# Attention and maxout feed-forward on one core: a re-planned order from the first folds on, and filler copies in the lead

## The chip, the cores and the metric

The kernel runs on 1 of the 8 cores of a Trainium2 chip. The metric is device microseconds (us) of one execution on that core. Three runs of the kernel before took 160.72, 161.04 and 161.48 us; their median is 161.04 us. One further execution was profiled.

## What is computed

```python
a = softmax(phi, axis=seq)                      # 8 batches, 8 heads, 576 rows, 32 memory slots
k_m, v_m = einsum('bhsm,bhsd->bhmd', a, k), the same with v      # head size 64
attn = softmax(q @ k_m.T / 8)                   # 576 x 32 per head
x = (attn @ v_m), heads side by side            # 4608 x 512
h = max(x @ w1, x @ w2, x @ w3)                 # 4608 x 768
out = h @ w_out                                 # 4608 x 512, float32
```

## The kernel before

**The algebra.** `attn @ v_m @ w` is computed as `attn @ (v_m @ w)`: the small v_m of a batch is first multiplied into the weights (called a fold, `fold`, L462), and the attention weights then go through the folded weights (`ffn1`, L513). The maxout is computed on differences: w1-w3 and w2-w3 are folded, h is the maximum of the two results and 0, and the part x @ w3 @ w_out comes back through a third folded matrix made of w3 @ w_out (`w3_o`, L197). The subtractions of w3 are done in place in the weights (`w_diff`, L218); batch 0 is folded before them, with an extra matmul of minus w3.

**The stages of a batch.** Loads of phi, k, v and q; an exponential of phi (`att_exp`, ScalarE); products of it with k and v (`att_kv`, TensorE, L256); their normalising (`att_kv_norm`) and transposing (`att_kv_t`, L315); scores from the transposed q (`att_q` is the transpose on VectorE, `att_score` the matmuls L351 and an exponential on ScalarE); the second softmax by a transpose, a sum, a reciprocal, a multiply and a transpose back; four folds; twelve `ffn1` groups of four matmuls over 576 columns, of which the even ones end in a relu and the odd ones in a maximum on VectorE; and the second feed-forward. For batches 0 and 1 that is `ffn2` (begun by `ffn2_begin`, L672, four matmuls); for the others it is done with seven block products instead of eight (`products`, L624), whose sums of blocks (`combine`, L549) run on GpSimd or VectorE.

**The order.** Nothing is scheduled for the program: `manual_schedule` is on, and one long string of words is issued word by word (L810 to L840). A word is a letter, a number and a batch: `F10@0` is ffn1 group 10 of batch 0. Each engine runs its instructions in the order of the words. The letters used in the text: L loads (0 phi, 1 k, 2 v, 3 q), J half of a q, Y weights; E exponential of phi; B products with k and v (B0 for k and B1 for v in batches 0 and 1, without a number for both); N normalise; K transpose; Q transpose of q; S scores; a, s, c, m, X the second softmax; D folds; F ffn1; t and T begin and end of ffn2; V the subtraction of w3; U and A sums of blocks of the weights and of the activations (batch 9 stands for w_out itself); P products; r packing of k; g sending an output; Z warm-up matmuls. An exclamation mark swaps the engine: ScalarE against VectorE for what empties PSUM, VectorE against GpSimd for V, U, A and m, GpSimd against ScalarE for r.

**PSUM.** There are eight banks. Each word that writes PSUM takes the next digit of a string (L143); D, F, B, and S take pairs (S two pairs). A word can start on a bank only when its earlier contents have been read.

**Loads and packing.** All loads but the first phi are issued from GpSimd's queue (POOL), in the order of the words, and the same queue holds GpSimd's computing instructions, so a waiting instruction holds back the loads behind it. k is loaded densely (tile ko, two buffers) and packed with a column of ones into the tile kvr (three buffers), from batch 2 on, by `pack` (L107 on GpSimd, L105 on ScalarE). v is loaded into kvr itself, q into qq (two buffers).

```python
        if swap:
            nc.scalar.copy(out=out_, in_=in_)
        else:
            nc.gpsimd.tensor_copy(out=out_, in_=in_)
```

Of the kernel before, what the change touches and what calls it, by code (L numbers as in the profile page):

```python
# [9 lines left out]
BF16 = mybir.dt.bfloat16  # L10
# [5 lines left out]
def kernel(  # L16
# [12 lines left out]
    nc = tc.nc  # L29

    B, H, S, D = q.shape
    M = phi.shape[-1]
    P = 128
# [11 lines left out]
    const = ctx.enter_context(tc.tile_pool(name="const", bufs=1))  # L45
# [18 lines left out]
    K1 = NP * NC * KS  # L64
# [20 lines left out]
    def load_ph(b):  # L85
        ph = inp.tile([P, NP, NC, M], FP32, name="ph", tag="ph")
        loaded.setdefault(b, {})["ph"] = ph
        dst = ph.rearrange("p j c m -> p j (c m)")
        if b == 0:
            for h in halves:  # L90
                nc.sync.dma_start(out=dst[:, h], in_=by_pair(phi, b)[:, h])
        else:
            nc.gpsimd.dma_start(out=dst, in_=by_pair(phi, b))

    def load_kv(b, i, h=slice(0, NP)):
        kv = vs[b % 3] if i else ks[b % 2]
        nc.gpsimd.dma_start(  # L97
            out=kv[:, h].rearrange("p j c d -> p j (c d)"),
            in_=by_pair((k, v)[i], b)[:, h],
        )  # L100

    def pack(b, swap):
        out_, in_ = krs[b % 3][:, :, :, 0:D], ks[b % 2]
# [5 lines that stand above are left out]
    def load_q(b, h=slice(0, NP)):  # L109
        if "q" not in loaded.setdefault(b, {}):  # L110
            loaded[b]["q"] = inp.tile([P, NP, NC, D], BF16, name="qq", tag="qq")
        nc.gpsimd.dma_start(  # L112
            out=loaded[b]["q"][:, h].rearrange("p j c d -> p j (c d)"),
            in_=by_pair(q, b)[:, h],
        )

    def load_w(i):
        w = (moe_w1, moe_w2, moe_w3)[i]
        nc.gpsimd.dma_start(  # L119
            out=w_sb[:, :, i], in_=w.rearrange("(j p) f -> p j f", p=P)  # L120
        )
# [3 lines left out]
    def load_wo():  # L125
        nc.gpsimd.dma_start(out=wo_sb, in_=moe_w_out.rearrange("(t p) c -> p t c", p=P))
# [3 lines left out]
    warm = const.tile([P, BANK], BF16, name="warm")  # L130
# [7 lines left out]
    for i in range(P // M):  # L138
# [4 lines left out]
    banks = iter(  # L143
        "".join(
            """
            00232204420145545045026406426402640264023462467420742602462062460264024603604206
            42604620642164646240624607402604260240402402420724062042642024204204260424026427
            402742002442072420426045026520026265260602406243352
            """.split()
        )  # L150
    )
# [1 line left out]
    def one_bank():  # L153
        return psum[:, int(next(banks))]
# [5 lines left out]
    def warm_up(n):  # L160

        po = one_bank()
        for _ in range(n):
            nc.tensor.matmul(  # L164
                po[:, 0:BANK], lhsT=warm[:, 0:P], rhs=warm, start=True, stop=True
            )
# [46 lines left out]
    def w_diff(n, swap):  # L213

        c, end = [(0, BANK), (BANK, DF), (2 * BANK, 2 * DF), (DF, 2 * BANK)][n]
        while c < end:
            e = min(end, (c // DF + 1) * DF)
            (nc.gpsimd if swap else nc.vector).tensor_tensor(  # L218
                out=w12[:, :, c:e],
                in0=w12[:, :, c:e],  # L220
                in1=w_sb[:, :, 2, c % DF : c % DF + e - c],
                op=ALU.subtract,
            )
            c = e
# [202 lines left out]
    def att_rec(b, g):  # L427
        x = st[b]["ts"][:, groups(g)]
        nc.vector.reciprocal(out=x, in_=x)  # L429
# [302 lines left out]
    def ffn2_last(b, c0):  # L732
# [18 lines left out]
        for i, (c, po) in enumerate(zip(cs, pos)):  # L751
# [13 lines left out]
            else:  # L765
                nc.scalar.copy(out=ot[:, c], in_=po)
                nc.scalar.dma_start(out=rows, in_=ot[:, c])

    def issue(b, n, swap):

        i = int(n[1:]) if len(n) > 1 else None
        {
            "I": lambda: [make_identity(nc, ident)]
            + [nc.gpsimd.memset(x[:, :, :, D:], 1.0) for x in krs],
            "Y": lambda: load_w(i) if i < 3 else load_wo(),
            "L": lambda: load_ph(b) if i == 0 else load_q(b) if i == 3 else load_kv(b, i - 1),
            "J": lambda: load_q(b, halves[i]),
            "H": lambda: load_kv(b, i % 2, halves[i // 2]),
            "h": lambda: load_kv(b, 0, slice(i, i + 1)),
            "r": lambda: pack(b, swap),  # L780
            "E": lambda: [att_exp(b, h) for h in (halves if b == 0 else [slice(0, NP)])],
            "B": lambda: att_kv(b, i),
            "N": lambda: att_kv_norm(b, swap, i),
            "K": lambda: att_kv_t(b, swap, i),
            "Q": lambda: att_q(b, i),
            "S": lambda: att_score(b),
            "a": lambda: att_t(b, i),
            "s": lambda: att_sum(b, i),
            "c": lambda: att_rec(b, i),
            "m": lambda: att_mul(b, i, swap),  # L790
            "X": lambda: (ones_mul if (b, i) in ONES else att_back)(b, i),
            "M": lambda: ones_sum(b, i),
            "R": lambda: ones_rec(b, i),
            "D": lambda: fold(b, i, swap),
            "F": lambda: ffn1(b, i, swap),
            "T": lambda: ffn2(b, i, swap),
            "U": lambda: combine_w(b, i, swap),
            "A": lambda: combine_a(b, i, not swap),
            "P": lambda: products(b, i, swap),
            "W": lambda: w3_t(i, swap),  # L800
            "g": lambda: send(i),
            "d": lambda: fold_begin(i),
            "t": lambda: ffn2_begin(b, i),
            "O": lambda: w3_o(i, swap),
            "V": lambda: w_diff(i, swap),
            "Z": lambda: warm_up(i),
        }[n[0]]()


    for w in """  # L810
        E@0 h2@0 h3@0 h0@0 h1@0 L3@0 Z25@0 B0@0 Y2@0 I@0 N0@0 Z2@0 K0@0! Q0@0 Q1@0 Z9@0 S@0 Z2@0
        M0@0 M1@0 R0@0 R1@0 W0@0 Y3@0 W1@0 W2@0 Z6@0 O1@0 H3@0 O3@0 O2@0 H1@0 X1@0 B1@0
        X0@0 N1@0 K1@0 O0@0 Y0@0 D1@0! D0@0! D3@0 F10@0 F0@0! F8@0 Y1@0 L0@1 L1@1 J0@1
        F2@0! F6@0 V0@0! D4@0! D2@0 E@1 J1@1 F4@0! F1@0 F5@0 L2@1 F3@0 F7@0 F9@0 L3@2
        F11@0 B0@1 N0@1! t1@0 L1@2 t2@0 Q1@1 Q0@1 T2@0 K0@1! V1@0 V3@0 T1@0 S@1 L0@2
        B1@1 U0@9! N1@1! M1@1 a0@1 R1@1 t3@0 K1@1! T3@0 L2@2 s0@1 L1@3 c0@1 V2@0 D0@1
        D1@1! L0@3 D2@1 L2@3 t0@0 r0@2 X1@1 m0@1! X0@1 T0@0 F10@1! Q0@2 F6@1 E@2 F7@1
        F0@1 g2@0 F11@1 L3@3 F1@1 D3@1 Q1@2 F2@1 B@2 U1@9 F4@1 L1@4 L0@4 N@2 F3@1 F8@1
        K@2 g1@0 F5@1 L2@4 S@2 F9@1 D1@2! t3@1 E@3 D0@2 D2@2 D3@2 L3@4 a@2 T3@1 s@2 U3@9
        T4@1! c@2 m@2! r0@3 X@2 B@3 F0@2 U0@2 N@3 F8@2! F6@2 K@3 U1@2 Q0@3 L1@5 F2@2  # L820
        L0@5 Q1@3 U3@2 F10@2 g0@0 F3@2 F4@2 F9@2 F11@2 U2@9 S@3 a@3 s@3 t2@1 c@3 g3@0
        D3@3 D2@3 L2@5 U2@2 D0@3 U0@3 t0@1 r0@4! E@4 F1@2 T0@1! U1@3 F5@2 T2@1! F7@2
        t1@1 m@3 L3@5 A0@2! X@3 L0@6 T1@1! F6@3 F4@3! D1@3! B@4 N@4 L1@6 A1@2! F0@3 Q1@4
        F2@3 Q0@4 L2@6 A2@2! F8@3 K@4! F7@3 P1@2! F1@3 S@4 P2@2 F10@3 D0@4 a@4 D1@4!
        P0@2 A3@2! s@4 c@4 F3@3 P4@2 E@5 r0@5! F11@3 F9@3 m@4 F5@3 L3@6 P5@2 A0@3! T4@3!
        A1@3! D3@4 B@5 X@4 N@5 D2@4 Q1@5 Q0@5 P6@2 F2@4 K@5 P3@2 F10@4! S@5 L1@7 P1@3!
        D2@5 D1@5! a@5 F11@4 P2@3 F8@4 s@5 c@5 U2@3 L0@7 F4@4! F0@4 F6@4 r0@6! L2@7 P0@3
        F1@4 F7@4 F9@4 P4@3 E@6 A2@3! A3@3! F3@4 F5@4 P3@3 D0@5 m@5 L3@7 U3@3 D3@5 B@6
        A0@4! A1@4! X@5 N@6 P5@3 F6@5 F8@5! Q0@6 r0@7 F2@5 Q1@6 F10@5 K@6! F9@5 U0@5
        F4@5 F7@5 P6@3! S@6 E@7 F3@5 P1@4 a@6 F5@5 F11@5 P2@4 D0@6 U0@4 B@7 D3@6 U2@4  # L830
        N@7 s@6 P0@4 A2@4! F0@5 F1@5 Q1@7 K@7! U1@4 A3@4! P4@4 D1@6! A0@5! D1@7! c@6
        D2@7! m@6 P3@4! U3@4 P5@4! D0@7 D2@6 D3@7 U2@6 Q0@7 X@6 T4@5 S@7 A1@5! A3@5!
        P6@4! F10@6 a@7 F6@6 s@7 F4@6 F11@6 F0@6 F7@6 c@7 P1@5 P2@5 F2@6! U2@5 F5@6 F3@6
        P0@5 U1@5 F1@6 m@7 F8@6 A2@5! X@7 P4@5 P3@5 F4@7 U0@6 U1@6 F10@7 U3@5 F9@6 P5@5!
        F5@7 F8@7 A0@6! P1@6! A1@6! F2@7 F6@7 F0@7 P6@5! U0@7 F7@7 F3@7 F1@7 P2@6! F11@7
        F9@7 A0@7 P0@6 A2@6! A1@7 P4@6 A3@6 U3@6! P1@7 P2@7 A2@7 P5@6 P3@6 U2@7! U1@7
        P4@7 P0@7! A3@7 P6@6 U3@7! P5@7 P3@7! P6@7! T4@7!
    """.split():
        n, b = w.rstrip("!").split("@")
        issue(int(b), n, w.endswith("!"))  # L840


# [28 lines left out]
```

## Time and profile before

| | us |
|---|---|
| median of three runs | 161.04 |
| profiled execution | 160.76 |
| span of that execution | 159.0 |
| TensorE busy (matmuls) | 149.6 |
| VectorE busy | 116.8 |
| GpSimd busy | 109.2 |
| ScalarE busy | 98.8 |

The span is what the profiler sees of the program; the execution's own time has 1.8 us more around it. PE is TensorE's matmuls, PEld its weight loads, DVE VectorE, ACT ScalarE, POOL GpSimd, SP the queue that sends most outputs. Matmuls are pipelined: the record of a 288-column matmul lasts 0.29 us, but they start 0.12 us apart, so a group of four takes PE 0.49 us and its result is there about 0.17 us later. The granted TensorE clock was full (1.00) throughout. In a row of the timeline the number in brackets is the idle time of the engine before it and what ended that.

### The profile page before, as it was taken

How to read it: one execution, taken by the hardware profiler on the slowest of the kernel's cores; microseconds unless marked ns; L12 is line 12 of the kernel's file. 1: busy time of each engine (PE TensorE's matmuls, PEld its weight loads, DVE VectorE, ACT ScalarE, POOL GpSimd, SP SyncE). 2: the span in 40 equal slices, each digit the busy share in tenths (PEclk: the TensorE clock that was granted, in tenths of full speed). 3: DMA queues.
4: the chain of work that ended last, by engine and by line, in shares of the span. 5: the costliest groups of instructions: out<-in, count | busy, mean ns of one | idle time of the engine just before them, and what ended most of it. 6: DMA issues, size and time to landing. Idle time of an engine off the chain costs nothing.

```text
span 159.0 us, 5179 instructions
## 1 busy us (share of the span) xinstructions
PE 149.6 (94%) x2218; PEld 100.3 (63%) x2228; DVE 116.8 (73%) x203; ACT 98.8 (62%) x142; POOL 109.2 (69%) x101
## 2 busy tenths in 40 slices
PE   6987798999798999999999999999999999999992
PEld 2442443574456538556776768887774888888871
DVE  2022803698988899787989688999998895679871
ACT  3205335723888699799699878886788826424110
POOL 7961102995039948889999999799969997890000
PEclk9999999999999999999999999999999999999999
DMA  5999999999999999999999999999303500332554
GB/s 150 168 199 209 205 210 211 281 207 210 207 281 225 298 236 243 307 262 214 323 246 277 213 255 284 278 239 246 111 0 136 200 4 0 132 132 70 177 187 164
DMA packets 22934, 31.78 MB, mean 200 GB/s; under 512 B 1152, under 2 KB 18560, under 8 KB 22912
## 3 DMA queue, kind: packets, MB, share of 16 engines
q0 software_dynamic: 16128, 21.43, 70.2%
q1 hardware_dynamic: 6064, 8.85, 15.8%
q10 hardware_dynamic: 720, 1.18, 2.2%
q8 instruction: 17, 0.28, 0.7%
q14 instruction: 5, 0.04, 0.1%
HBM read 39.32 MB, written 9.44 MB: 307 GB/s over the span
## 4 chain that ended last, share of the span: by engine, by line
PE 72%; DMA 19%; POOL 5%; issue 1%; ACT 1%; POOLq 0%
PE psum L513 26%; PE psum L624 24%; DMA w_sb<-in_moe_w_dram 13%; DMA kvr<-in_v_dram 6%; PE psum L462 5%; PE psum L690 4%; PE psum L672 3%; PE psum L256 3%; PE psum L699 2%; PE psum L351 2%; POOL ko L97 1%; PE psum L708 1%; POOL qq L112 1%; POOL w_sb L119 1%; PE psum L753 1%
## 5 line engine op out<-in xcount | busy, mean ns | idle before, releaser
L513 PE MATMUL psum<-hx,wp 128*128 128x288 bf16 x384 | 53.7, 286 | 0.7 <-DVE wp L181 0.3
L513 PEld LDWEIGHTS <-wp 128*128 128x128 bf16 x384 | 36.6, 98 | 12.3 <-issue 1.5
L526 DVE TENSOR_TENSOR hx<-psum,h 128x576 bf16<-128x576 f32 x48 | 34.1, 744 | 3.3 <-PE psum L513 2.7
L177 ACT CAST wp<-psum 128x1024 bf16<-128x1024 f32 (+1 forms) x30 | 28.2, 993 | 2.7 <-PE psum L462 2.3
L175 ACT ACTIVATE h<-psum 128x576 bf16<-128x576 f32 x38 | 23.8, 651 | 8.9 <-PE psum L513 8.7
L624 PEld LDWEIGHTS <-hx 128*128 128x128 bf16 x192 | 18.4, 98 | 3.5 <-issue 0.9
L360 ACT ACTIVATE e<-psum 128x576 bf16<-128x576 f32 x16 | 9.5, 649 | 7.5 <-PE psum L351 7.5
L549 POOL TENSOR_TENSOR w_sb<-hx 128x1024 bf16<-128x1024 bf16 x5 | 10.6, 2130 | 4.0 <-DVE hx L526 2.6
L164 PE MATMUL psum<-warm 128*128 128x512 bf16 x42 | 11.8, 435 | 1.4 <-DVE warm L131 1.2
L330 DVE STREAM_TRANSPOSE qT<-qq 128x576 f32<-128x576 f32 x16 | 11.6, 757 | 2.0 <-DMA qq<-in_q_dram 2.0
L624 PEld LDWEIGHTS <-w_sb 128*128 128x128 bf16 x120 | 11.4, 98 | 2.5 <-issue 0.7
L107 POOL COPY kvr<-ko 128x2304 bf16<-128x2304 bf16 x3 | 6.3, 2108 | 7.7 <-DMA ko<-in_k_dram 7.7
L218 POOL TENSOR_TENSOR w_sb<-w_sb 128x2048 bf16<-128x2048 bf16 x1 | 4.1, 4065 | 10.4 <-PE psum L462 10.4
L436 POOL TENSOR_TENSOR t<-t,sm 128x1152 bf16<-128x1152 bf16 x5 | 10.6, 2127 | 0.6 <-DVE sm L429 0.5
L549 POOL TENSOR_TENSOR w_sb<-w_sb,hx 128x1024 bf16<-128x1024 bf16 x5 | 10.6, 2128 | 0.3
L234 ACT ACTIVATE e<-ph 128x1152 bf16<-128x1152 f32 (+1 forms) x9 | 9.6, 1063 | 1.8 <-DMA ph<-in_phi_dram 1.8
L549 POOL TENSOR_TENSOR hx<-hx 128x1024 bf16<-128x1024 bf16 x5 | 10.7, 2130 | 0.0
L549 POOL TENSOR_TENSOR twb<-wp 128x256 bf16<-128x256 bf16 x11 | 7.3, 670 | 3.9 <-ACT wp L177 3.9
L624 PE MATMUL psum<-w3T,hx 128*128 128x256 bf16 x72 | 9.8, 273 | 0.0
L624 PE MATMUL psum<-wo_sb,hx 128*128 128x256 bf16 x72 | 9.8, 273 | 0.0
L656 DVE TENSOR_TENSOR ot<-psum,snap 128x512 f32<-128x512 f32 x12 | 8.3, 689 | 1.9 <-PE psum L624 1.3
L97 POOL DMA_DIRECT2D ko<-in_k_dram x11 | 7.7, 700 | 2.9 <-DMA qq<-in_q_dram 1.5
(106 smaller groups left out, 272.2 us busy)
## 6 DMA issues: line engine op xcount, KB each, us to landing
out_dram<-ot SPq DMA_DIRECT2D x8, 512.0 KB, 4.2
qq<-in_q_dram POOLq DMA_DIRECT2D x7, 576.0 KB, 13.5
ph<-in_phi_dram POOLq DMA_DIRECT2D x7, 576.0 KB, 15.3
ko<-in_k_dram POOLq DMA_DIRECT2D x7, 576.0 KB, 16.1
kvr<-in_v_dram POOLq DMA_DIRECT2D x7, 576.0 KB, 18.0
out_dram<-ot SPq DMA_DIRECT2D x14, 256.0 KB, 2.2
w_sb<-in_moe_w_dram POOLq DMA_DIRECT2D x3, 768.0 KB, 17.9
out_dram<-ot ACTq DMA_DIRECT2D x4, 256.0 KB, 6.2
```

Of the source, the lines that this page charges most:

```text
L97: nc.gpsimd.dma_start(out=kv[:, h].rearrange("p j c d -> p j (c d)"), in_=by_pair((k, v)[i], b)[:, h],)
L164: nc.tensor.matmul(po[:, 0:BANK], lhsT=warm[:, 0:P], rhs=warm, start=True, stop=True)
L175: nc.scalar.activation(out=out_, in_=in_, func=AF.Relu)
L177: nc.scalar.copy(out=out_, in_=in_)
L234: nc.scalar.activation(out=s["e"][:, js], in_=loaded[b]["ph"][:, js], func=AF.Exp)
L330: nc.vector.transpose(out=s["qT"][:, j].rearrange("p j c r e -> p (j c r e)").bitcast(FP32), in_=loaded[b]["q"][:, j].rearrange("p j c d - ...
L360: nc.scalar.activation(out=e2[:, a].rearrange("p (t r c) -> p t r c", t=2, c=NC), in_=sc[a][:, :, 0:SH].rearrange("p t (c r) -> p t r c", ...
L436: (nc.vector if swap else nc.gpsimd).tensor_tensor(out=t, in0=t, in1=x.to_broadcast(list(t.shape)), op=ALU.mult,)
L513: nc.tensor.matmul(acc[:, h, 0:SH], lhsT=wps[b][:, g, w * DF + ft * P : w * DF + (ft + 1) * P], rhs=attn[:, g, c0 : c0 + SH], start=(g == ...
L526: nc.vector.tensor_tensor(out=hT[:, row(ft), (b % 2) * S : (b % 2 + 1) * S].rearrange("p (h n) -> p h n", h=2), in0=a, in1=s["h1", ft], op ...
L549: eng.tensor_tensor(out=out_, in0=in0, in1=in1, op=op)
L624: nc.tensor.matmul(po[:, q * CH : (q + 1) * CH], lhsT=lhs(k, q), rhs=rhs(k), start=(i < 3 and k == 0 and q == 0), stop=(k == KT and q == 1 ...
```

## The change

The words up to `D3@0` (the third fold of batch 0) and their banks stay. Two things change.

First, four words `p` are added ahead of and in the lead: 41 copies on VectorE, and 8, 30 and 14 on ScalarE. Each copies one column (128 partitions, 1 element) from `warm` into a tile that nobody reads. They lengthen the two engines' instruction streams, so that another instruction is the last of the engine's first block of instructions.

Second, everything after `D3@0` stands in another order, with another bank string and other marks for the engine. The words themselves are the same. Among the moves: `F8`, `F10`, `F0`, `F4` of batch 0 all go to VectorE for their relu; `t0@0` moves ahead of `B0@1`; `V1@0` goes to GpSimd and `V0@0` to VectorE (before: the other way round); the loads of batch 2 go out as phi, k, v, q (before: q, k, phi, v); `U2@9` and `U0@9` run on GpSimd between `L3@2` and `L1@3`; `L1@3` is followed at once by the packing `r0@2`, with `L0@3`, `L2@3` and `L3@3` behind it; `N@2`, `K@2` go to ScalarE; `r0@7` goes to ScalarE.

```diff
-            00232204420145545045026406426402640264023462467420742602462062460264024603604206
...
+            00232204420145545045026402640240624602467406065460260246042064064204620465026406
...
+    pads = [const.tile([P, 64], BF16, name=f"pads{i}") for i in range(2)]
+    cols = [iter(range(64)) for _ in range(2)]
+
+    def pad(n, swap):
+
+        for i in (next(cols[swap]) for _ in range(n)):
+            (nc.vector.tensor_copy if swap else nc.scalar.copy)(
+                out=pads[swap][:, i : i + 1], in_=warm[:, 0:1]
+            )
...
+            "p": lambda: pad(i, int(swap)),
...
-        E@0 h2@0 h3@0 h0@0 h1@0 L3@0 Z25@0 B0@0 Y2@0 I@0 N0@0 Z2@0 K0@0! Q0@0 Q1@0 Z9@0 S@0 Z2@0
+        p41@0! p8@0 E@0 p30@0 h2@0 h3@0 h0@0 h1@0 L3@0 Z25@0 B0@0 Y2@0 I@0 N0@0 Z2@0 K0@0! p14@0 Q0@0 Q1@0 Z9@0 S@0 Z2@0
         M0@0 M1@0 R0@0 R1@0 W0@0 Y3@0 W1@0 W2@0 Z6@0 O1@0 H3@0 O3@0 O2@0 H1@0 X1@0 B1@0
-        X0@0 N1@0 K1@0 O0@0 Y0@0 D1@0! D0@0! D3@0 F10@0 F0@0! F8@0 Y1@0 L0@1 L1@1 J0@1
-        F2@0! F6@0 V0@0! D4@0! D2@0 E@1 J1@1 F4@0! F1@0 F5@0 L2@1 F3@0 F7@0 F9@0 L3@2
-        F11@0 B0@1 N0@1! t1@0 L1@2 t2@0 Q1@1 Q0@1 T2@0 K0@1! V1@0 V3@0 T1@0 S@1 L0@2
-        B1@1 U0@9! N1@1! M1@1 a0@1 R1@1 t3@0 K1@1! T3@0 L2@2 s0@1 L1@3 c0@1 V2@0 D0@1
-        D1@1! L0@3 D2@1 L2@3 t0@0 r0@2 X1@1 m0@1! X0@1 T0@0 F10@1! Q0@2 F6@1 E@2 F7@1
-        F0@1 g2@0 F11@1 L3@3 F1@1 D3@1 Q1@2 F2@1 B@2 U1@9 F4@1 L1@4 L0@4 N@2 F3@1 F8@1
-        K@2 g1@0 F5@1 L2@4 S@2 F9@1 D1@2! t3@1 E@3 D0@2 D2@2 D3@2 L3@4 a@2 T3@1 s@2 U3@9
...
+        X0@0 N1@0 K1@0 O0@0 Y0@0 D1@0! D0@0! D3@0 F8@0! F10@0! Y1@0 L0@1 L1@1 F0@0!
+        F4@0! F2@0 D2@0 D4@0! J0@1 F1@0 V1@0! F3@0 F6@0 J1@1 L2@1 L0@2 F7@0 L1@2 E@1
+        F11@0 F5@0 L2@2 L3@2 F9@0 t0@0 B0@1 N0@1! t2@0 T2@0! K0@1! Q0@1 t1@0 Q1@1 V2@0
+        U2@9 S@1 T1@0 V3@0 B1@1 U0@9 N1@1! V0@0 a0@1 M1@1 L1@3 r0@2 R1@1 t3@0 K1@1! s0@1
+        L0@3 c0@1 T0@0! D0@1 m0@1! X1@1 X0@1 D2@1! D1@1! T3@0! F4@1! F2@1! E@2 F5@1
+        F10@1 F3@1 F6@1 B@2 N@2! F7@1 F0@1 Q1@2 K@2! F8@1 Q0@2 F11@1 g1@0 g2@0 F9@1 L2@3
+        S@2 F1@1 a@2 L3@3 U1@9 L1@4 s@2 c@2 D3@1 D0@2 D3@2 D1@2! t3@1 U3@9 r0@3 E@3 m@2!
+        U0@2 D2@2 L0@4 T4@1! X@2 T3@1 F4@2! g3@0 B@3 F10@2 L2@4 N@3 U1@2 F2@2 L3@4 F11@2
...
```

## Prediction, as put on record before the changed kernel ran

> **What bounds the kernel now.** I read the page's busy shares, then the same by stretches, then TensorE's waits, then the loads' landings.
>
> ```profile
> PE 149.6 (94%) x2218; PEld 100.3 (63%) x2228; DVE 116.8 (73%) x203; ACT 98.8 (62%) x142; POOL 109.2 (69%) x101
> ...
> DMA  5999999999999999999999999999303500332554
> ```
>
> ```profile
> 25.00:41.00 16.00, 14.67 (x301) 8.45 (x302) 11.99 (x19) 8.43 (x15) 10.73 (x10) 1.00 1.19 227
> 41.00:60.00 19.00, 18.42 (x346) 10.13 (x336) 17.13 (x28) 16.27 (x25) 11.09 (x9) 1.00 1.17 251
> 60.00:156.00 96.00, 95.68 (x1347) 71.83 (x1340) 80.83 (x136) 65.21 (x92) 76.75 (x59) 1.00 0.75 190
> ```
>
> The columns after the length are the busy times of PE, PEld, DVE, ACT and POOL. TensorE idles 1.33 us from 25 to 41, 0.58 from 41 to 60 and 0.32 in the 96 us after. Its work stays the same (the same words), so from 25 us on no order can gain more than 2.2 us, and from 60 on an order can only lose. The largest holes:
>
> ```profile
> PE psum L256 <- DMA kvr<-in_v_dram: 0.8, 1, 0.8
> ...
> PE psum L513 <- DVE wp L181: 0.3, 1, 0.3
> ...
> PE psum L513 <- DVE hx L526: 0.2, 1, 0.2
> PE psum L256 <- ACT wp L177: 0.2, 1, 0.2
> ```
>
> The first is B1@1 waiting for v of batch 1. The loads behind it, from the DMA issues (size, us to landing):
>
> ```profile
> kvr<-in_v_dram POOLq DMA_DIRECT2D x1, 576.0 KB, 8.9
> ...
> qq<-in_q_dram POOLq DMA_DIRECT2D x1, 576.0 KB, 11.0
> ...
> ko<-in_k_dram POOLq DMA_DIRECT2D x1, 576.0 KB, 13.1
> ...
> ph<-in_phi_dram POOLq DMA_DIRECT2D x1, 576.0 KB, 13.9
> ...
> kvr<-in_v_dram POOLq DMA_DIRECT2D x1, 576.0 KB, 15.8
> ```
>
> Issued at 31.68, 32.43, 33.16, 33.89 and 34.63, they land at 40.6, 43.4, 46.3, 47.8 and 50.4: one after the other, 2.6 to 2.9 us each and 1.5 for phi, with the DMA engines full. So a landing here is set by what is queued ahead, not by when it was issued.
>
> **The change, part by part.**
>
> *Copies in the lead.* ScalarE's timeline (start, length, operation, and the pause before it) has the pauses and, in its last two rows, the price:
>
> ```profile
> 3.71 0.68 ACT L234 ACTIVATE e<-ph 128x576 bf16<-128x576 f32 x1 [1.68 <-DMA ph<-in_phi_dram]
> ...
> 10.71 0.37 ACT L177 COPY kvt<-psum 128x256 bf16<-128x256 bf16 x1 [5.47 <-PE psum L315]
> 13.56 1.19 ACT L360 ACTIVATE e<-psum 128x576 bf16<-128x576 f32 x2 [2.47 <-PE psum L351]
> ...
> 36.98 0.63 ACT L305 ACTIVATE kvn<-psum,rden 128x128 bf16<-128x128 f32 x2 [4.12 <-DVE rden L276]
> ...
> 41.40 0.52 ACT L282 ACTIVATE kvn<-psum,rden 128x64 bf16<-128x64 f32 x2 [0.28 <-PE psum L256]
> ```
>
> Two operations of 64 columns start 0.21 us apart, of 128 columns 0.27; carried on to one column that is 0.16 (an estimate). 8, 30 and 14 copies are then 1.3, 4.8 and 2.2 us, inside the pauses of 1.68, 5.47 and 2.47. At 0.21 each, the upper bound, the kvt copy comes 0.8 late (hidden: the scores start at 12.55) and the exponentials 1.3 late; of that the 0.95 us in which TensorE waits for w_out before 19.36 covers all but 0.35. On VectorE 41 copies at 0.06 (a memset of one column) to 0.17 (the reciprocal of two) are 2.5 to 7.0 us in a pause of 7.61 after 1.91. What they can win: a stall where the instruction blocks end. But the waits of VectorE and ScalarE name a releasing operation everywhere, none "issue"; nothing to win. Taken: 0, between -0.2 (the smallest waits that the list shows) and +0.35.
>
> *Up to B1@1.* F8 and F10 need D1 alone, so the 0.3 wait for D0's eviction goes. New ones come: four relus in a row on VectorE (one per 0.67, TensorE makes one per 0.49) delay D4's bank by 0.3, and F1 waits 0.35 for D2's copy on ScalarE, which stands behind F2's relu. Late next is nothing: V1 takes half of V0's 4.07 us on GpSimd, so the loads behind it go out about 2.6 us earlier, but v of batch 1 has the same loads ahead of it and lands at 40.6 as before. TensorE, which got there at 39.80 and waited 0.77, now does t0@0 first (four matmuls, 0.97 on the chain), gets there at about 40.2 and waits 0.4. B1@1 starts at 40.6 in both, with 0.97 us more work behind it.
>
> *Loads of batch 2.* phi, k, v, q in the place of q, k, phi, v: 40.6 + 1.5 + 2.9 + 2.6 + 2.8, so k lands at 45.0, v at 47.6 and q at 50.4. r0@2 (2.1 us) starts at 45.0 in the place of 46.4 and ends at 47.1. L1@3 goes out at about 36.2 (V1, six loads of 0.75 and 3.3 us of U2@9 and U0@9 are ahead of it; before 36.04), and the three loads behind the packing at 47.2 to 49.4, while the queue has work until k of batch 3, past 52: the DMA engines do not run dry. B@2 comes at 41.35 + M1 0.35 + t3 0.97 + K1 and T0 0.93 + three folds 0.94 + a 0.16 wait for T0's bank + T3 0.87 + six F 2.94 = 48.6: it finds v and the packed k. Before it started at 50.59.
>
> *From B@2 to the first F of batch 2.* The covers in this stretch are short. K@2 needs N@2, now on ScalarE: reciprocal 0.17, four scalings 1.06, hand-overs 0.25, so 1.5 after B@2, of which F7 and F0 cover 1.0: a wait of 0.5. The two q transposes on VectorE (1.44) end at 52.2 and S@2 comes at 52.4: no wait, but the maxima of F11 and F9 are behind them, and F1 waits 0.1 for F11's bank. D3@1 waits 0.2 for the exponential of the first half of S@2. t3@1 needs the bank of D3@1, whose copy takes ScalarE 1.0; three folds cover it but for 0.3. From S@2's end to the end of X@2 it was 54.15 to 60.30, 6.15 us; now 5.8 of work and 0.6 of those waits cover it: 0. With the 0.16, TensorE waits 1.3 here where it waited 0.58.
>
> *After that.* The same words, bank reuse as short as before at its shortest (0.87 to 0.98 us of work after a score group's end in both orders), GpSimd with one packing less (2.1). The 96 us had 0.32 of waits; I take 0, between -0.3 and +2.9 (the rate of 41 to 60).
>
> **Sum.** -0.97 + (1.3 - 0.58) = -0.25 us. On the profiled 160.76 that is 160.5; the median stands 0.28 above the profiled execution, so 160.8, and I say 160.7. 0.5%, 0.8 us, is what a measurement of this kernel can tell from no change.
>
> **Rivals.**
> 1. *The waits behind B@2 do not open.* For it: they are sums of hand-overs, and a late start of one hides the next. Then the 0.97 and all of the 0.58 are won: 161.04 - 1.55 = 159.5.
> 2. *q of batch 2 last.* Slower: q stands in the place that v had, but on VectorE Q1@2 now stands ahead of F11, F9, F1 and the second softmax, all in order. Every 0.1 us that q lands after 50.7 is 0.1 us of the end. Two loads at the 3.6 us that k of batch 3 took (50.4 to 54.0) in the place of 2.8 make it 52.0, and the time 162.1; from 51.7 on it is slower. Against it: outputs, which slowed that load, are sent later in the new order.
> 3. *The saturated part.* 60 to 156 leaves no room; at the waits of 41 to 60 the time is 160.8 + 2.9 = 163.7, at a third of them 161.8.
> 4. *The copies hold up the first loads.* In this kernel VectorE copies out of PSUM only, never from SBUF to SBUF, and GpSimd issues the four k loads in 2.32 us beside VectorE's memsets. If each of the 41 copies kept GpSimd from issuing for its 0.06 us, all loads, queued back to back until 50.4, come 2.5 us later, B1@1 too: 163.3; it decides from 18 copies on. The Trainium skill (SBUF — State Buffer, "Who interferes with whom") says that a VectorE copy from SBUF to SBUF can take the port pair that it shares with GpSimd, and that descriptors of loads issued from GpSimd then wait. By that rule the sum is 163.3, by the rows 160.7; no row of before shows such a copy, and one-element copies are the least likely to do it.
>
> **How the numbers follow.** The forecast (160.3 to 161.2) 0.41; rival 1 0.26; rival 2 0.17; rival 3 0.10, seven tenths of it beyond 0.5%; rival 4 0.06. Faster 0.26, same 0.41 + 0.03 = 0.44, slower 0.17 + 0.07 + 0.06 = 0.30. The range goes from rival 1's 159.5 to 162.6, past rival 2 and the lower half of rival 3; the likeliest case alone has 160.3 to 161.2.
>
> **What would show it.** Right: no late kvt or exponential in the lead; B1@1 at 40.6 still waiting for v; B@2 near 48.6 without a DMA wait; K@2 waiting about 0.5 for ScalarE; F4@2 near 59.4. Wrong: the first k loads landing after 8.6, a VectorE transpose waiting for q past 50.7, or more than 0.6 us of TensorE idle after 60.

## Result and profile after

| | before | after |
|---|---|---|
| median, us (22 runs each, one chip) | 160.66 | 161.29 |
| profiled execution | 160.76 | 161.31 |
| its span | 159.0 | 159.2 |
| time outside the span, median | 1.79 | 2.16 |

The ratio is 1.0037, with a 95% interval from 1.0025 to 1.0048: slower by 0.63 us. I had forecast 0.25 faster. It is less than the 0.5% within which I would call two times the same, but the interval leaves out 1. Of the 0.63 us, 0.37 lie outside the span, where my sum had no term.

The page of the changed kernel has these busy times:

```profile
PE 150.3 (94%) x2228; PEld 100.3 (63%) x2228; DVE 120.0 (75%) x238; ACT 105.6 (66%) x203; POOL 107.1 (67%) x100
```

By the page VectorE and ScalarE have 35 and 61 more instructions: the 41 and 52 copies, and what the changed marks move from the one to the other. The same stretches as before the change (length, then PE, PEld, DVE, ACT and POOL):

```profile
25.00:41.00 16.00, 15.65 (x289) 8.80 (x287) 13.78 (x20) 7.74 (x14) 10.60 (x10) 1.00 1.17 245
41.00:60.00 19.00, 18.07 (x315) 9.87 (x299) 16.74 (x24) 16.75 (x29) 13.26 (x11) 1.00 1.19 235
60.00:156.00 96.00, 95.89 (x1380) 71.91 (x1379) 80.24 (x132) 67.19 (x96) 72.58 (x57) 1.00 0.75 189
```

TensorE idles 0.35 us from 25 to 41 (1.33 before), 0.93 from 41 to 60 (0.58 before) and 0.11 after 60. By this view the new order wins 0.84 us; the clock says otherwise. The busy time of overlapping matmuls is not their pace, and that is the first lesson of this case: the starts of the scores (the 32 matmuls of L351, one row per batch in TensorE's timeline) are the safer ruler.

| from the start of the scores of ... to ..., us | before | after |
|---|---|---|
| batch 1 (39.33, 39.37) to batch 3 | 25.71 | 25.56 |
| batch 3 to batch 5 | 26.80 | 26.87 |
| batch 5 to batch 7 | 30.39 | 30.66 |
| batch 7 to the last product (L753) | 32.18 | 32.18 |

The same words lie between these marks in both orders, apart from a few. Those are of equal length but for one pair: between batch 1 and batch 3 the old order has t0@0 (0.97 us) where the new one has T1@0 (0.87). So the rearranged middle won 0.15, of which 0.10 is work that has moved ahead of the first mark. Ahead of that mark the new order wins as well: from the first product of w3 and w_out to the scores of batch 1 it takes 19.67 us (from 19.70 to 39.37) and the old order 19.97 (from 19.36 to 39.33), although the new order has 0.10 more work there. That doesn't show in the table, because these products start 0.33 later in this execution; in the one execution of the new order in which they start as early as before (19.37), it takes 19.91.

0.27 was lost between batch 5 and batch 7, where the list of waits has no entry at all. From 25 to 156 it has these three:

```profile
PE psum L672 <- ACT wp L177: 0.4, 1, 0.4
...
PE psum L315 <- ACT kvn L305: 0.3, 1, 0.3
PE psum L513 <- ACT wp L177: 0.3, 1, 0.3
```

The wait for v of batch 1 is gone; the first two are t3@1 and K@2, which the prediction had priced at 0.3 and 0.5; the third is F1@0, priced at 0.35. The first two stand like this in TensorE's timeline (start, length, and the pause before the row in brackets), with F4@2, the first F of batch 2, in the last row:

```profile
48.55 0.81 PE L256 MATMUL psum<-kvr,e 64*32 64x130 bf16 x72
...
50.77 0.28 PE L315 MATMUL psum<-ident,kvn 128*128 128x128 bf16 x2 [0.27 <-ACT kvn L305]
...
55.28 1.02 PE L672 MATMUL psum<-wo_sb,hx 128*128 128x512 bf16 x4 [0.37 <-ACT wp L177]
...
59.41 0.65 PE L513 MATMUL psum<-hx,wp 128*128 128x288 bf16 x4
```

The loads from v of batch 1 on (us from issue to landing) are issued at 29.64, 30.39, 31.13, 31.86 and 32.59:

```profile
kvr<-in_v_dram POOLq DMA_DIRECT2D x1, 576.0 KB, 10.5
...
ph<-in_phi_dram POOLq DMA_DIRECT2D x1, 576.0 KB, 11.6
...
ko<-in_k_dram POOLq DMA_DIRECT2D x1, 576.0 KB, 13.4
...
kvr<-in_v_dram POOLq DMA_DIRECT2D x1, 576.0 KB, 15.5
...
qq<-in_q_dram POOLq DMA_DIRECT2D x1, 576.0 KB, 17.6
```

They land at 40.1, 42.0, 44.5, 47.4 and 50.2. In the lead the copies fill ScalarE's pauses (the first row has 30 of its 52) and VectorE's (last row) and make nothing late: the copy of kvt starts at 10.47 (10.71 before), the exponentials at 13.54 (13.56).

```profile
5.13 2.88 ACT L775 COPY pads<-warm 128x1 bf16<-128x1 bf16 x30
10.47 0.37 ACT L177 COPY kvt<-psum 128x256 bf16<-128x256 bf16 x1 [2.46 <-PE psum L315]
...
1.93 2.58 DVE L775 COPY pads<-warm 128x1 bf16<-128x1 bf16 x41
```

### The profile page after: what moved, and what is told of

Read it like the earlier page. It is cut to its first block, busy times and chain, and to the rows that moved or that the text cites. A ratio compares the mean times of both kernels' runs of the same rounds, so it can differ in the third digit from the quotient of the medians.

```text
span 159.2 us, 5280 instructions
## 1 busy us (share of the span) xinstructions
PE 150.3 (94%) x2228; PEld 100.3 (63%) x2228; DVE 120.0 (75%) x238; ACT 105.6 (66%) x203; POOL 107.1 (67%) x100
## 4 chain that ended last, share of the span: by engine, by line
PE 80%; DMA 9%; ACT 3%; POOL 3%; DVE 2%; issue 1%; ACTq 0%; DVEq 0%; POOLq 0%
PE psum L513 28%; PE psum L624 24%; DMA wo_sb<-in_moe_w_out_dram 9%; PE psum L690 5%; PE psum L672 5%; PE psum L462 4%; PE psum L256 4%; PE psum L197 3%; PE psum L699 2%; PE psum L351 2%; POOL ko L97 1%; ACT wp L177 1%; DVE hx L526 1%; PE psum L708 1%; PE psum L753 1%
## 5 line engine op out<-in xcount | busy, mean ns | idle before, releaser
L526 DVE TENSOR_TENSOR hx<-psum,h 128x576 bf16<-128x576 f32 x48 | 34.6, 747 | 5.7 <-PE psum L513 4.6
L175 ACT ACTIVATE h<-psum 128x576 bf16<-128x576 f32 x37 | 22.8, 661 | 12.1 <-PE psum L513 11.6
L177 ACT CAST wp<-psum 128x1024 bf16<-128x1024 f32 (+1 forms) x28 | 26.5, 990 | 2.0 <-PE psum L462 1.8
L638 ACT COPY snap<-psum 128x512 f32<-128x512 f32 x9 | 5.3, 588 | 8.3 <-PE psum L624 8.2
L112 POOL DMA_DIRECT2D qq<-in_q_dram x9 | 6.9, 769 | 3.6 <-DMA w_sb<-in_moe_w_dram 3.6
L690 PE MATMUL psum<-wo_sb,hx 128*128 128x512 bf16 x34 | 9.2, 380 | 0.0
```

The costliest lines, as they stand in the source:

```text
L175: nc.scalar.activation(out=out_, in_=in_, func=AF.Relu)
L526: nc.vector.tensor_tensor(out=hT[:, row(ft), (b % 2) * S : (b % 2 + 1) * S].rearrange("p (h n) -> p h n", h=2), in0=a, in1=s["h1", ft], op ...
L690: nc.tensor.matmul(po, lhsT=hT[:, row(fc), c0 : c0 + P], rhs=wo_sb[:, fc, :], start=(n == 0 and not early), stop=False,)
```

## The copies, the order, and the end of the program

The first four kernels part the copies from the order. Theories: the copies cost at the end of the program because of where VectorE's last instruction block ends (then another number of copies changes it); or the copies cost something else; or the order costs it all.

**The new order without copies** (the `p` words taken out):

```diff
-        p41@0! p8@0 E@0 p30@0 h2@0 h3@0 ... K0@0! p14@0 Q0@0
+        E@0 h2@0 h3@0 ... K0@0! Q0@0
```

> The changed order without the four words p. Theory (end of a block): the 41 copies push a third block end of VectorE's instructions into the last instructions of the program, which costs 0.37 us after the span; without them the execution's own time is 1.76 us longer than the span, as before, in the place of 2.13. Theory (lead): the copies also cost the 0.33 us by which w3 and w_out land later; without them the first w3o matmul starts at 19.4 in the place of 19.7. Both together: 160.6, level with the kernel before (160.66). Rival (the order costs): 161.3 as with the copies, and 19.4 or 19.7 is chance.

**The copies in the old order** (the kernel before, with the four `p` words):

```diff
-        E@0 h2@0 h3@0 ... K0@0! Q0@0
+        p41@0! p8@0 E@0 p30@0 h2@0 h3@0 ... K0@0! p14@0 Q0@0
```

> The kernel before with the four words p and nothing else. VectorE then has one instruction more than in the changed kernel. Theory (end of a block, and lead): slower than before by 0.3 to 0.7 us (0.37 outside the span, up to 0.33 in the lead). Rival (the order costs): the same as before within 0.1 us.

**60 and 10 copies on VectorE in the place of 41** (ScalarE's 52 kept):

```diff
-        p41@0! p8@0 E@0
+        p60@0! p8@0 E@0
```

```diff
-        p41@0! p8@0 E@0
+        p10@0! p8@0 E@0
```

> The changed kernel with 60 copies on VectorE in the place of 41: the third block end comes 19 instructions earlier, well before the end, and its block is loaded while the kernel runs. Theory (end of a block): more copies make it faster, by 0.37 us, and the time outside the span goes back to 1.76. Theory that each copy costs: slower by a little, and 2.13 or more outside the span.

> The changed kernel with 10 copies on VectorE in the place of 41, ScalarE's 52 kept: the third block end lies behind the program. Theory (end of a block): 1.76 outside the span, 0.37 us faster than the changed kernel, so 160.9; if VectorE's copies are also what delays the first loads, 160.6. If ScalarE's copies did either, 161.3.

Measured (ratio to the kernel before on the same chip; 12 runs each, but 33 in the first row; the last row is the result above, with its own runs of the kernel before):

| order | copies on VectorE, ScalarE | median, us | ratio and 95% interval | outside the span |
|---|---|---|---|---|
| old | 0, 0 | 160.60 | 1 | 1.79 |
| new | 0, 0 | 160.85 | 1.0016 [1.0004, 1.0027] | 1.79 |
| old | 41, 52 | 160.94 | 1.0021 [1.0008, 1.0034] | 1.79 |
| new | 60, 52 | 160.82 | 1.0011 [0.9998, 1.0024] | 1.80 |
| new | 10, 52 | 160.97 | 1.0020 [1.0008, 1.0033] | 1.78 |
| new (the change) | 41, 52 | 161.29 | 1.0037 [1.0025, 1.0048] | 2.16 |

More copies than 41 are cheaper, and so are fewer: the 0.37 outside the span are not the price of the copies. The theory on the lead fell: without copies the products of w3 and w_out start at 19.95 and not at 19.4, later than with them (19.70). So the new order without copies came between the two forecasts, 160.6 and 161.3.

The traces show what the 0.37 hang on. Instructions come in packets of 8 KB on a DMA queue of their own (the page has five of them, 0.04 MB). I count an engine's recorded instructions with its semaphore waits, which the page leaves out: VectorE has 280 before and 317 in the changed kernel. Which engine a packet is for is inferred from this count: in all the kernels packets follow VectorE's 59th to 73rd instruction, its 189th to 197th and about its 320th, that is every 128 or so. I call these places the ends of its blocks. The changed kernel's third packet for VectorE is fetched at 160.8 us, behind all 317 and after the span's last instruction. With 60 copies it follows the 320th, at 148.2, and the kernel's page has a sixth:

```profile
q14 instruction: 6, 0.05, 0.1%
```

With 10 or no copies there is no third packet. In the old order with the copies VectorE has 321 recorded instructions. The 320th, a flush among the last instructions of the program, starts 0.44 us after the end of the one before it (0.09 in the kernel before), the packet comes at 159.1, and from the first of the last products (L753) to the end of the span it takes 4.79 us in the place of 4.57. So 0.22 of that kernel's 0.34 us (by its interval 0.13 to 0.55) can be seen there, inside the span; the rest is not accounted for. So this part is shown: a block of VectorE that ends in the last instructions of the program costs 0.37 us outside the span in the changed kernel.

It left 0.25 us for the new order alone, and the loss between batch 5 and batch 7 unexplained.

## Four experiments on the rest

**Two of six relus to VectorE.** Right behind the scores of batch 5 the new order has six F in a row (F3, F10, F8, F6, F9, F4 of batch 4), which take 3.31 us in the changed kernel where TensorE needs 2.94. My theory was ScalarE's pace.

```diff
-        S@5 F3@4 F10@4 F8@4 F6@4 a@5 F9@4 L2@7 U0@4 F4@4 s@5
+        S@5 F3@4 F10@4! F8@4 F6@4 a@5 F9@4 L2@7 U0@4 F4@4! s@5
```

> The new order without the copies, and the relus of F10 and F4 of batch 4 (two of the six F after the scores of batch 5) on VectorE in the place of ScalarE. Theory (the run of six F is held to ScalarE's pace: four relus and two exponentials, 3.31 us where TensorE needs 2.94): from the scores of batch 5 to those of batch 7 it takes 30.4 us in the place of 30.63, and the time is 160.60 (160.85 less 0.25). Rival (the loss lies elsewhere, or VectorE now delays the transpose behind the scores of batch 5): 160.85 or more, the stretch 30.6.

Measured: 1.0040 [1.0017, 1.0064]. The six F take 3.32 us, batch 5 to batch 7 takes 30.81. The theory falls: on VectorE the relu of F10 comes behind the maximum of F3, 1.86 us after the start of the scores; on ScalarE, in the changed kernel, it was 1.95.

**The old order from the scores of batch 5 on** (banks renamed; F10 of batch 4, which before comes ahead of these scores, right behind them):

```diff
-        S@5 F3@4 F10@4 F8@4 F6@4 a@5 F9@4 ...
+        S@5 F10@4! P1@3! D2@5 D1@5! a@5 F11@4 P2@3 F8@4 ...
```

> The new order without the copies up to the scores of batch 5, then the order of before to the end (F10 of batch 4, which before has ahead of these scores, right behind them; banks renamed to fit). Theory (the new order wins in its first half and loses 0.27 between the scores of batch 5 and 7): 160.6, and the stretch takes 30.3 to 30.4. Rival (the new order's loss sits in its lead or first half): 160.85, whatever the tail.

Measured: 1.0044 [1.0028, 1.0060], 31.16 us from batch 5 to batch 7. It decides nothing: the joint makes waits of its own (one of 0.3 for a relu).

**Another bank for F9.** F9 takes the pair of banks that F10 wrote two F earlier; I took the 0.3 us for that. From F9 on the pairs 01 and 67 exchange names:

```diff
-            24026402460346406426046204620624126421426426442604206420647024204204042042064206
-            126412646226416246204260560650262626406246526567574
+            24026402460346406426046204620624126421426426442604260426041624264264642642604260
+            720472040220470240264206506056202020460240520501514
```

> The new order without the copies, and from F9 of batch 4 on the bank pairs 01 and 67 exchange names to the end. F9 of batch 4 then no longer takes the pair that F10 of batch 4 wrote two F earlier (its relu ends about 0.3 us after TensorE could start F9), but the pair of F3, which VectorE has emptied by then; F4 takes F10's. Nothing else changes. Theory (the 0.25 us lost between the scores of batch 5 and 7 is F9 waiting for its bank, hidden in the records because the matmuls overlap): the six F take 2.95 to 3.05 us in the place of 3.31 to 3.39, the stretch 30.35 in the place of 30.65, the time 160.55 (160.85 less 0.3). Rival (F4 now waits as long for F10's relu, or the run is held by something else): 160.85. If the late w_out in the lead belongs to the new order and is no chance, the products of w3 and w_out start at 19.55 to 19.95 again.

Measured: 1.0019 [1.0003, 1.0035], the same as without the swap (1.0016). The six F take 3.04 us, as forecast. But so they do in the kernel that it was made from: without copies they take 3.05, and only with ScalarE's copies 3.31. I had compared both kernels, this one and the one with the relus, with the wrong trace. The gain never reaches the scores of batch 7 either: from batch 6 on the kernels without copies lose 0.24 where those with VectorE's copies don't. Two places, each with its own group of copies: that was the clue.

**The loads of batch 2 in the old order** (q, k, phi, v), in the new order without copies:

```diff
-        ... J1@1 L2@1 L0@2 F7@0 L1@2 E@1 F11@0 F5@0 L2@2 L3@2 F9@0
+        ... J1@1 L2@1 L3@2 F7@0 L1@2 E@1 F11@0 F5@0 L0@2 L2@2 F9@0
```

> The new order without the copies, the loads of batch 2 again as q, k, phi, v. If a landing is set by what is queued ahead, v of batch 2 lands at 50.4 in the place of 47.6, and its products, which start at 48.6, wait 1.8 us for it; the time is 160.85 + 1.3 to 1.8 = 162.2 to 162.7, less if the waits behind are swallowed. Rival (the load order is worth nothing by itself, the products are held by something else): 160.9, no wait for v.

Measured: 1.0136 [1.0111, 1.0162], 1.9 us more than the same kernel with the new load order (1.0016), a little above the forecast. v of batch 2 lands at 50.4, as forecast, and TensorE waits for it until 50.50:

```profile
PE psum L256 <- DMA kvr<-in_v_dram: 2.0, 1, 2.0
```

(Its profiled execution is longer still than the median; the granted clock was 0.91 from 41 to 60 there.) So that part of the prediction stands: a landing is set by what is queued ahead, and the new place of B@2 needs the new order of the loads. By itself it wins nothing, it only doesn't lose.

## Where the instruction blocks end

The theory left: an engine stands still when it comes to the end of a block, and TensorE loses by it where that engine is wanted at once. ScalarE's copies move the second end of ScalarE into the six F, VectorE's copies move the second end of VectorE away from the products of batch 7. It says what the two missing combinations must do.

**10 copies on VectorE, none on ScalarE; and none on VectorE, 52 on ScalarE:**

```diff
-        p41@0! p8@0 E@0 p30@0 h2@0 h3@0 ... K0@0! p14@0 Q0@0
+        p10@0! E@0 h2@0 h3@0 ... K0@0! Q0@0
```

```diff
-        p41@0! p8@0 E@0 p30@0 h2@0 h3@0 ... K0@0! p14@0 Q0@0
+        p8@0 E@0 p30@0 h2@0 h3@0 ... K0@0! p14@0 Q0@0
```

> The changed kernel with 10 copies on VectorE in the place of 41, and without the 52 on ScalarE. Theory (an engine stands still for 0.2 to 0.4 us each time it comes to about its 64th, 192nd and 320th instruction, where its block of instructions ends, and TensorE loses about 0.25 where that engine is then wanted at once): ScalarE's second end is at 122.5, as without copies, harmless; VectorE's second end moves from 113 (where it holds the maximum that the products of batch 7 wait for) to 108, harmless; no third end. So the stretch from the scores of batch 5 to those of batch 6 is 14.27 as without copies (14.53 with ScalarE's), and from batch 6 to 7 it is 16.1 to 16.2 as with VectorE's copies (16.36 without): 30.4 together, and the time is 160.6 (160.85 less 0.24). Rival (the differences are chance, or belong to the run of F and its banks): 30.63, 160.85.

> The changed kernel without the 41 copies on VectorE, the 52 on ScalarE kept. Theory of the block ends: both bad places are hit: ScalarE's second end falls behind the two exponentials of batch 5 (93.6), so that the relu of F10 of batch 4 starts 1.95 us after the scores instead of 1.67 and the run of six F takes 3.3; VectorE's second end falls at 113. From the scores of batch 5 to 6 it is 14.53, from 6 to 7 16.36: 30.9 together, and the time is 161.1 (160.85 plus 0.27), the slowest of the four combinations; nothing outside the span beyond 1.8. Rival: 30.63, 160.85.

Measured: 1.0001 [0.9988, 1.0014] and 1.0034 [1.0020, 1.0048]. All kernels of the new order side by side (us between the starts of the scores):

| copies on VectorE, ScalarE | batch 5 to 6 | batch 6 to 7 | ratio |
|---|---|---|---|
| 0, 0 | 14.27 | 16.36 | 1.0016 |
| 10, 0 | 14.27 | 16.18 | 1.0001 |
| 0, 52 | 14.54 | 16.35 | 1.0034 |
| 10, 52 | 14.54 | 16.18 | 1.0020 |
| 60, 52 | 14.53 | 16.12 | 1.0011 |
| 41, 52 (the change) | 14.54 | 16.12 | 1.0037 |

The first stretch hangs on ScalarE's copies alone (0.27 us), the second on VectorE's alone (0.17 to 0.24). The stalls themselves can be read. ScalarE of the changed kernel, behind the scores of batch 5 (the exponentials, then the relus of the six F):

```profile
92.37 1.19 ACT L360 ACTIVATE e<-psum 128x576 bf16<-128x576 f32 x2 [0.68 <-PE psum L351]
93.74 2.53 ACT L175 ACTIVATE h<-psum 128x576 bf16<-128x576 f32 x4 [0.17 <-ACT e L360]
```

and with 10 copies on VectorE and none on ScalarE:

```profile
92.28 1.19 ACT L360 ACTIVATE e<-psum 128x576 bf16<-128x576 f32 x2 [0.68 <-PE psum L351]
93.36 1.74 ACT L175 ACTIVATE h<-psum 128x576 bf16<-128x576 f32 x3
```

The first relu starts 1.37 us after the exponentials in the one, 1.08 in the other: ScalarE stood still for 0.29, and the bracket names ScalarE's own instruction as what it waited for. TensorE, the six F of the changed kernel and the folds behind them:

```profile
92.20 3.38 PE L513 MATMUL psum<-hx,wp 128*128 128x288 bf16 x24
95.51 0.62 PE L462 MATMUL psum<-w_sb,kvt 64*32 64x512 bf16 x16
```

and with 10 copies on VectorE and none on ScalarE:

```profile
92.11 3.11 PE L513 MATMUL psum<-hx,wp 128*128 128x288 bf16 x24
95.16 0.62 PE L462 MATMUL psum<-w_sb,kvt 64*32 64x512 bf16 x16
```

3.31 us against 3.05. The wait sits between matmuls that overlap in the records, so no list of waits has it. The other place, VectorE without copies (the new order, no `p` words):

```profile
113.04 0.76 DVE L526 TENSOR_TENSOR hx<-psum,h 128x576 bf16<-128x576 f32 x1 [0.94 <-ACT snap L638]
```

and in the changed kernel, where this end has moved to 95:

```profile
112.68 0.76 DVE L526 TENSOR_TENSOR hx<-psum,h 128x576 bf16<-128x576 f32 x1 [0.57 <-PE psum L513]
```

The maximum, whose matmuls start at 111.91 and 111.92, comes 0.37 us later, and B@7, which takes a bank after it, 0.24 later (113.85 against 113.61). Here the bracket names an instruction of ScalarE that has nothing to do with it.

In both places the late instruction is the engine's 192nd recorded one: the first relu is ScalarE's 192nd in all four kernels of the table with ScalarE's copies, the maximum is VectorE's 192nd in the two without VectorE's. The run with two relus on VectorE confirms it without any copies. There the maximum is VectorE's 193rd, it starts 6.36 us after the scores of batch 6 (6.35 in the changed kernel, 6.73 in the new order without copies), and from batch 6 to 7 it takes 16.12.

Most ends cost nothing, and at many no pause can be seen: in none of the kernels does VectorE's or ScalarE's 64th instruction start more than 0.04 us after the one before it, and with 60 copies VectorE's 192nd starts 0.03 after. So an engine does not stand still each time, as the theory had it. The first ends of both engines, at 50.2 and 57.1 in the new order without copies and at 17 to 21 us with them, make no difference between the scores of batch 1 and 3: 25.56 us in both. So what the copies do in the lead, they do for nothing. The old order has its second ends at 110 and 127, and takes 30.39 us from batch 5 to 7 with them there; the copies move them to 89 and 97, and it takes 30.39 again.

## What the order itself is worth

**One of its moves alone, in the kernel before**: t0@0 ahead of the products with k of batch 1, in a free bank.

```diff
-        F11@0 B0@1 N0@1! t1@0 L1@2 t2@0 ...
+        F11@0 t0@0 B0@1 N0@1! t1@0 L1@2 t2@0 ...
...
-        D1@1! L0@3 D2@1 L2@3 t0@0 r0@2 X1@1
+        D1@1! L0@3 D2@1 L2@3 r0@2 X1@1
```

> The kernel before with one word moved: the begin t0 of batch 0 (four matmuls, 0.97 us of TensorE on the chain) goes ahead of the products with k of batch 1, so that it is done before the wait for v of batch 1; its bank is one that is free there. Theory of the prediction (TensorE's wait for v is filled with work that had to be done anyway): 0.77 us less idle before the products with v; of that all is won where the second softmax of batch 1 is ready in time for its first F, so 159.85 to 160.4. Rival (what t0 covered behind the softmax of batch 1 now shows as a wait of about the same length): 160.6.

Measured: 1.0118 [1.0073, 1.0163], well outside both forecasts. The scores of batch 1 start at 40.95 in the place of 39.33: t0 first waits 0.6 us for a maximum on VectorE, then it is itself ahead of them, and the sum of exponentials behind waits for the later scores:

```profile
PE psum L372 <- ACT e L360: 0.7, 1, 0.7
PE psum L672 <- DVE hx L526: 0.6, 1, 0.6
```

I had looked only at the wait for v, which is behind the scores, and not at what t0 pushes back ahead of them.

**The pair of moves**: t0@0 behind t1@0, and T1@0 behind the scores of batch 1, as in the new order.

```diff
-        F11@0 B0@1 N0@1! t1@0 L1@2 t2@0 Q1@1 Q0@1 T2@0 K0@1! V1@0 V3@0 T1@0 S@1 L0@2
+        F11@0 B0@1 N0@1! t1@0 t0@0 L1@2 t2@0 Q1@1 Q0@1 T2@0 K0@1! V1@0 V3@0 S@1 T1@0 L0@2
```

> The kernel before with the two words around the wait for v of batch 1 that the new order moves: the begin t0 of batch 0 goes ahead (behind t1), and the end T1 of batch 0 goes behind the scores of batch 1, so that these scores start when they did (39.3 to 39.5) and TensorE comes to the products with v 0.1 us later than it did only by t0 less T1, plus T1: at about 40.8, no wait. Theory (the gain at the wait for v is open to the old order too, but the cover that t0 gave the second softmax of batch 1 is gone, so that its folds and first F wait): the idle time from 25 to 41 falls by 0.6 to 0.9, that from 41 to 60 rises by 0.3 to 0.9; the time is 160.3 to 160.9. Rival (moving t0 is worth its full 0.77 also here): 159.9. The products of w3 and w_out start at 19.3 to 19.4 if the lead belongs to the order.

Measured: 1.0038 [1.0024, 1.0052], 161.27 us against 160.52: worse than either theory's time. Without T1 between K0 and the scores these wait 0.5 for the copy of kvt, and behind, a first F waits 0.5 for folded weights:

```profile
PE psum L351 <- ACT kvt L177: 0.5, 1, 0.5
PE psum L513 <- ACT wp L177: 0.5, 1, 0.5
```

TensorE's idle time falls by 0.27 from 25 to 41 and rises by 0.37 from 41 to 60. The gain at the wait for v is not open to two moves alone.

**The wait for v is no constant.** In the profiled execution of the kernel before:

```profile
39.33 0.47 PE L351 MATMUL psum<-qT,kvt 32*32 32x288 bf16 x32
40.58 0.75 PE L256 MATMUL psum<-kvr,e 64*32 64x64 bf16 x72 [0.77 <-DMA kvr<-in_v_dram]
```

and in that of the old order with copies:

```profile
39.31 0.49 PE L351 MATMUL psum<-qT,kvt 32*32 32x288 bf16 x32
40.08 0.75 PE L256 MATMUL psum<-kvr,e 64*32 64x64 bf16 x72 [0.28 <-DMA kvr<-in_v_dram]
```

The same order, the scores at the same moment, and v lands 0.5 earlier. From batch 1 to batch 3 the old order takes 25.71 in the one and 25.26 in the other, the new order 25.56 to 25.57 in all nine profiles that keep its first half and its loads. So the new order takes away a wait of 0.3 to 0.8 and pays about 0.6 behind B@2 (K@2's 0.27 and t3@1's 0.37): it wins 0.15 against the execution that I had worked from and loses 0.30 against the other. Its best form, 10 copies and no bad block end, is the kernel before again: 1.0001.

## Why the prediction was wrong

The change is +0.63 us. The runs give: order without bad block ends 0.0 (1.0001, give or take 0.2), ScalarE's second end in the six F +0.27, VectorE's third end at the end of the program +0.37. That is +0.64; with an uncertainty of 0.2 it is luck that it comes so near. I had forecast -0.25: of the 0.88 between forecast and result, 0.64 are block ends in bad places, which the step on the copies had at nothing, and 0.25 is the gain of the order, which is not there. Point by point, by the steps of the prediction:

- **Copies in the lead: this is the step that failed.** Its timing held (nothing late; a copy on ScalarE takes 0.10 us and not the estimated 0.16, on VectorE 0.063). But it was taken at 0, between -0.2 and +0.35, and the runs show +0.34 for the copies against the new order without them by the ratios (1.0037 and 1.0016), +0.40 by the terms (+0.27 + 0.37 - 0.24). That this is near the upper bound is luck: the bound was for exponentials that come late in the lead, and they did not. I asked only what the moved first ends could win, and not where the second and third ends go. That could have been counted: before, packets follow VectorE's 70th and 195th recorded instruction (at 50.5 and 110.1), so the next is due at about the 320th, and 280 instructions and 41 copies are 321. The reason that I gave, that the waits name a releasing operation everywhere, was a misreading. An end can show as an engine that waits for its own last instruction, and one such row, at ScalarE's 192nd recorded instruction, stood in the trace of before (the relus at 124 to 126). The row alone is no proof of an end: in the old order with copies one of 0.27 stands at ScalarE's 248th.

```profile
124.22 0.65 ACT L175 ACTIVATE h<-psum 128x576 bf16<-128x576 f32 x1 [0.22 <-PE psum L513]
125.06 1.82 ACT L175 ACTIVATE h<-psum 128x576 bf16<-128x576 f32 x3 [0.19 <-ACT h L175]
```

- **The time around the span** was carried over as 1.8. It is 2.16 in the changed kernel: a term that was missing, not one of a wrong size.
- **Up to B1@1.** B1@1 starts at 40.74 (forecast 40.6), but not at v: v lands at 40.14 and TensorE is busy without a pause until B1@1. The work that was moved ahead fills the wait wholly. The wait for D0's copy is gone as forecast, and F1 waits 0.26 (0.35). That the 0.77 was one execution's value and not the kernel's, the step did not ask.
- **Loads of batch 2.** k 44.5, v 47.4, q 50.2, forecast 45.0, 47.6, 50.4; the packing at 44.66 (45.0); B@2 at 48.55 (48.6, though the terms of that sum add up to 48.51), without a DMA wait. Right, and the run with the old order of loads shows the reason right.
- **B@2 to the first F of batch 2.** K@2 waits 0.27 (0.5), t3@1 0.37 (0.3), F4@2 comes at 59.41 (59.4). The idle time from 41 to 60 is 0.93 where I had 1.3. The middle as a whole, -0.15 by the scores against a sum of -0.25, was nearly right in the profiled pair; over many executions the new order at its best is level with the old one (1.0001). The base was off too: the kernel before was taken at 161.04, from three runs, and has 160.66 in 22.
- **After that: 0, between -0.3 and +2.9.** By the list of waits it is 0; by the scores it is +0.34: 0.27 is the block end, and the 0.07 between batch 3 and 5 stay unexplained. Bank reuse, for which I looked there, cost nothing: the swap of banks changed no time.
- **The rivals.** The waits behind B@2 did open (1). q of batch 2 landed at 50.2, and its transposes start at 50.74 behind a maximum (2). The saturated part has its loss, but not the one that I priced (3). GpSimd issued the first four k loads in 2.33 us (2.32 before) beside VectorE's 41 copies: no sign that these kept it off (4).

The Trainium skill (Runtime: NRT & Kernel Launch, "Instruction fetch mechanics") says that crossing a block boundary costs one tail-bump of a DMA and is mostly hidden. The blocks of the Trainium skill are of 16 KiB; the packets counted here for VectorE and ScalarE are of 8 KB. Most ends here are hidden, as it says. Three were not, at 0.2 to 0.4 us each, in a kernel whose changes are worth no more than that.

## What to carry to other kernels

Where a kernel is tuned to tenths of a microsecond, every added or removed instruction moves all later block ends of its engine. Count each engine's instructions and see what stands at those places, the end of the program among them. Then measure an order with two or three different numbers of idle copies before judging it. Measure progress by the starts of recurring landmarks rather than by idle time, which overlapping matmuls hide; and take a DMA wait from several executions before building on its size.

## What was not expected of the hardware

- VectorE and ScalarE came 0.37 and 0.29 us late to their 192nd recorded instruction, a few instructions ahead of an 8 KB packet on the instruction queue, where other kernels show no pause there. Why they do, no run here shows.
- A third block end in VectorE's last instructions costs 0.37 us outside the span (2.16 against 1.79), or 0.22 inside it (4.79 against 4.57 from the last products to the end).
- Where DMA has no part and the block ends stand alike, the stretches between scores repeat within 0.03 us from one kernel to the next. What varies lies ahead of 41 us: v of batch 1 lands between 40.1 and 40.6 in the profiles above, and the products of w3 and w_out start between 19.34 and 20.11, in the old order (19.34 to 19.79) as in the new (19.37 to 20.11), with the same words up to there apart from the copies. What sets it stayed open.
